# Attention and max-out feed-forward on one core: q and k loaded six tokens to a partition, w1 and w2 loaded over 128 partitions

## The chip, the cores and the metric

The kernel runs on one core of a Trainium2 chip. The metric is the device time of one execution in microseconds. Five executions of the kernel before took 218.94 to 220.14 us, with a median of 219.47 us. In the profile the engines are PE (TensorE, the matrix engine; PEld is its weight load), DVE (VectorE), ACT (ScalarE), POOL (GpSimd) and SP (SyncE, which here only issues DMAs). An engine's name with a q (SPq, PEq) stands for its instruction queue.

## What is computed

The inputs are q, k and v of shape [4, 8, 768, 64] (batch, heads, tokens, head size), three weight matrices, and a flag for each head. A flagged head attends causally to all earlier tokens. Any other head sees only the first 4 tokens and a window of 64. In this draw three of the eight heads are flagged (0, 2 and 6). All data is float32.

```python
def _attn_ref(q, k, v, is_retrieval, n_sink, window):
    scores = scale * np.matmul(q, k.transpose(0, 1, 3, 2))
    ...
    stream_keep = causal & (is_sink | in_win)
    ...
    a = np.exp(scores)
    a = a / (np.sum(a, axis=-1, keepdims=True) + 1e-09)
    return np.matmul(a, v).astype(np.float32)

def _moe_ref(x, w1, w2, w_out):
    return (np.maximum(x @ w1, x @ w2) @ w_out).astype(np.float32)
```

Between the two, the attention output is laid out as x with 4 * 768 = 3072 rows of tokens and 8 * 64 = 512 columns, head h in columns 64h to 64h + 63. w1 and w2 are [512, 1024], w_out is [1024, 512].

## The kernel before, in words

**The order of the heads.** The kernel sorts the heads on the chip (lines 280 to 295): the flagged ones first. Each *slot* 0 to 7 then holds a head, and `perm` holds which. If at most three heads are flagged (they are, here), the first branch at line 672 runs: SP loads the eight head numbers into registers (line 673), and the function `run` works on slots, slots 0 to 2 with the full causal triangle and 3 to 7 with the narrow band. Every load of q, k and v is addressed by the register of its slot (line 541). So the x that the attention writes has its columns in the order of the slots, and the rows of w1 and w2 are loaded in that same order (line 366), 64 rows at a time, each half into 64 partitions.

**Attention.** The function `pair` treats two slots of one batch; there are 4 batches of 4 pairs, 16 pairs. A pair loads q, k and v with two DMAs each (96 DMAs of 192 KB). The load puts token n * 128 + p on partition p, so a partition receives six separate rows of 64 floats. POOL casts each tile to bf16 (line 555; `qb` for q and k, line 574 `vb` for v). PE transposes q and k in six blocks of 128 tokens (line 563) into a PSUM bank (`mm`), and DVE or ACT copies the bank to `qt` (line 567, one copy) and `kz` (line 572, one copy for each head). The helper `copy` records these copies as line 255 on DVE and POOL, and as line 253 on ACT. Then, for each head, come scores on PE (line 435), the exponential on ACT (442), the mask product on DVE (451), the product with v on PE (507, 517), and the normalisation on DVE (524, 525), which writes the head's 64 columns of `xs`. After both heads of a pair, PE transposes the pair's 128 columns (601) and a copy puts them in `xt` (603).

**Feed-forward.** max(a, b) is computed as relu(a - b) + b. So `wd_bf` = w1 - w2 (line 384), and `wm_bf` = w2 @ w_out, which is made once on PE (lines 393 and 404). For each batch, in two halves of 384 tokens, `dense` computes relu(x @ wd) (lines 617, 624, 626), and then x @ wm + relu(...) @ w_out into one PSUM bank (636 and 642), copies it out (646) and stores it (649). `dense(b)` waits for all four `xt` copies of its batch and for the prepared weights.

**What sets the order.** Nothing is scheduled at run time: `Plan` holds a list of operations, each with its cost on the engines that may do it, a priority, the buffers it needs and the operations it waits for, and `schedule` (line 65) simulates them in time. It gives each operation to an engine and emits all of them in the order of their planned starts. Each engine, and SP's queue of DMA issues, then runs its instructions in exactly that order. A planned DMA takes its size over its `rate`; the loads of q, k and v are planned at 0.225 (MB per us), w1 and w2 at 0.37. The loads of pair r have priority r, and the 16 loads of w1 and w2 have 2.5, so they stand between the loads of pairs 2 and 3. Nine `ld` tiles take the loads of three pairs. PSUM has three `sc` banks, two `po` and three `mm`; the transposes, the feed-forward and the preparation of the weights share the three `mm` banks.

Of the kernel before, what the change touches and what calls it, by code (L numbers as in the profile page):

```python
# [149 lines left out]
def kernel(  # L150
# [61 lines left out]
    perm = tl("perm", [128, H + 4], I32)  # L212
    nsf = tl("nsf", [128, H], F32)
# [52 lines left out]
    with tc.manual_schedule():  # L266
# [27 lines left out]
        V.tensor_copy(out=perm[:, H:H + 1], in_=nr)  # L294
        V.tensor_scalar_mul(out=far0, in0=far, scalar1=nsink)

    def run(full, head, rows, flags):
# [59 lines left out]
        def weights(prio):  # L357
            for i, name in enumerate(("w2", "w1")):
                for c in range(4):
                    for hh in (range(2) if rows else (None,)):  # L360
                        def f(e, name=name, c=c, hh=hh):
                            if hh is None:
                                load_weight(name, c)
                            else:
                                arr = {"w1": moe_w1, "w2": moe_w2}[name].rearrange("(h d) f -> h d f", d=D)
                                nc.sync.dma_start(  # L366
                                    out=w_raw[{"w1": 0, "w2": 1}[name]][64 * hh:64 * hh + 64, c, :],
                                    in_=arr[bass.ds(head(2 * c + hh), 1)].rearrange("o d f -> (o d) f"))
                        d_w[name, c, hh or 0] = P.op(
                            f, {"SP": 0.5}, prio=prio + 0.1 * i + 0.01 * c,  # L370
                            size=0.524 if hh is None else 0.262, rate=0.37)
            return {(n, c): [o for (a, x, _), o in d_w.items() if (a, x) == (n, c)] for n in ("w1", "w2") for c in range(4)}
# [56 lines left out]
        xs, xt, xt_ops = {}, {}, {}  # L429
# [24 lines left out]
        def head_ops(b, s, hh, qt, kz, vb, tops, ov, sink, r):  # L454
# [67 lines left out]
            def norm(e):  # L522
                p3 = po.t[:, 0:NB * (D + 1)].rearrange("p (n e) -> p n e", e=D + 1)
                V.reciprocal(out=rz.t, in_=p3[:, :, D])
                V.tensor_tensor(out=xs[b].t[:, :, s * D:(s + 1) * D], in0=p3[:, :, 0:D],  # L525
                                in1=rz.t.unsqueeze(2).to_broadcast([128, NB, D]), op=ALU.mult)
            return P.op(norm, {"DVE": 0.68}, [prev], [po, rz, xs[b]], prio=hr)

        def pair(b, p):
            r = b * HP + p  # L530
            s0 = 2 * p
            if p == 0:
                xs[b], xt[b], xt_ops[b] = Buf(xs_p), Buf(xt_p), []
            raws, loads = [], []
            for i, src in enumerate((q, k, v)):
                t = Buf(ld)
                raws.append(t)
                if rows:
                    two = []
                    for hh in range(2):  # L540
                        two.append(P.op(lambda e, t=t, src=src, hh=hh: nc.sync.dma_start(  # L541
                            out=t.t[:, hh], in_=src[b, bass.ds(head(s0 + hh), 1)].rearrange(
                                "o (n p) d -> p (o n) d", p=128)),
                            {"SP": 0.5}, (), [t], prio=r + 0.01 * i, size=0.197, rate=0.225))
                    loads.append(two)
                else:
                    loads.append([P.op(lambda e, t=t, src=src: nc.sync.dma_start(
                        out=t.t, in_=src[b, s0:s0 + 2].rearrange("h (n p) d -> p h n d", p=128)),
                        {"SP": 0.45}, (), [t], prio=r + 0.01 * i, size=0.393, rate=0.225)])
# [3 lines left out]
            for i in range(2):  # L553
# [12 lines left out]
                if i == 0:  # L566
                    tops.append(P.op(lambda e, bk=bk: copy(e, qt.t, bk.t.bitcast(BF16)[:, 0:S]),
                                     {"DVE": 0.475, "ACT": 0.69}, [o], [bk, qt], prio=r))
                else:
                    for hh in range(2):  # L570
                        kops.append(P.op(lambda e, bk=bk, hh=hh: copy(
                            e, kz.t[64 * hh:64 * hh + 64, hh, :], bk.t.bitcast(BF16)[64 * hh:64 * hh + 64, 0:S]),
                            {"DVE": 0.475, "ACT": 0.69}, [o] + init, [bk, kz], prio=r + 0.1 * hh))
# [140 lines left out]
```

## Time and profile before

| what | value |
|---|---|
| median of 5 executions | 219.47 us |
| the profiled execution | 219.0 us |
| its span in the profile | 217.1 us |
| mean granted PE clock | 0.97 of full speed |
| busy: PE, ACT, DVE, POOL | 186.0, 136.3, 102.9, 60.1 us |
| DMA packets, and those under 512 B | 81263, 76112 |
| loads of q, k and v | 96 DMAs of 192 KB, 18.9 MB |
| loads of w1 and w2 | 16 DMAs of 256 KB, 4.2 MB |
| copies from PSUM to `kz`, DVE and ACT | 17 of 551 ns, 15 of 793 ns |
| copies from PSUM to `qt`, DVE and ACT | 12 of 552 ns, 4 of 809 ns |

The profile covers the span; 1.9 us of the profiled execution lie outside it. A busy time is the union of an engine's instructions, and for matrix products the ends are modelled. Where a copy has two lines in the profile (253 and 255), the tile's name says which copy it is.

### The profile page before, as it was taken

Reading aid. Unit: us, or ns where it says so; the run is one execution under the profiler, and the core shown is the slowest. Engines: PE = TensorE matmul, PEld = TensorE weight load, DVE = VectorE, ACT = ScalarE, POOL = GpSimd, SP = SyncE. Lnnn points to the kernel's source line nnn. Section 1 sums busy time; section 2 is a strip of 40 time slices with the busy share of each in tenths; the row PEclk is TensorE's granted clock in tenths of the full one; section 3 lists DMA queues with packets and bytes.
Section 4 is the critical chain, followed back from the end, with each engine's and each line's share of the span. In section 5 each row is a group of like instructions: output and inputs, shape, how many; then the busy total and the mean of one; then the engine's idle time right before and its main releaser. Section 6 shows DMA issues by size and latency. Waiting matters only on the chain.

```text
span 217.1 us, 4707 instructions
## 1 busy us (share of the span) xinstructions
PE 186.0 (86%) x1700; PEld 117.0 (54%) x1700; DVE 102.9 (47%) x269; ACT 136.3 (63%) x262; POOL 60.1 (28%) x117
## 2 busy tenths in 40 slices
PE   0029767699789998999999999999999999999990
PEld 0027546535567776667676677645445454554540
DVE  3886867532978898969898468400000000000000
ACT  0739878427988988978998887625436262442621
POOL 1473420656446455644636200000000000000000
PEclk9999995769999999999999999999999999999997
DMA  5999999999999999999996111012021121202121
GB/s 168 312 222 219 221 246 248 228 194 222 219 194 226 180 225 202 224 226 227 234 238 145 51 50 51 2 53 97 0 97 48 61 87 46 100 3 97 48 91 66
DMA packets 81263, 31.85 MB, mean 147 GB/s; under 512 B 76112, under 2 KB 76112, under 8 KB 81232
## 3 DMA queue, kind: packets, MB, share of 16 engines
q1 hardware_dynamic: 81232, 31.47, 64.9%
q8 instruction: 15, 0.25, 0.5%
q14 instruction: 16, 0.13, 0.2%
HBM read 25.17 MB, written 6.29 MB: 145 GB/s over the span
## 4 chain that ended last, share of the span: by engine, by line
PE 55%; DMA 14%; SPq 11%; DVE 5%; ACT 5%; issue 4%; POOL 3%; POOLq 0%; ACTq 0%; DVEq 0%
PE mm L636 17%; PE mm L617 16%; SPq L541 9%; PE mm L642 8%; DMA raw<-in_moe_w_dram 7%; PE sc L435 6%; DMA ld<-in_v_dram 3%; PE po L507 3%; DMA ld<-in_k_dram 2%; PE mm L563 2%; ACT at L442 2%; ACT kz L253 2%; DVE kz L255 2%; DMA ir<-in_is_retrieval_dram 1%; SPq L366 1%
## 5 line engine op out<-in xcount | busy, mean ns | idle before, releaser
L636 PE MATMUL mm<-wo_bf,raw 128*128 128x512 bf16 x192 | 46.3, 379 | 0.0
L617 PE MATMUL mm<-xt,wd_bf 128*128 128x384 bf16 x256 | 46.0, 326 | 0.0
L435 PE MATMUL sc<-qt,kz 128*128 128x256 bf16 (+3 forms) x240 | 41.0, 270 | 5.4 <-ACT at L442 2.2
L253 ACT COPY ot<-mm 128x512 f32<-128x512 f32 x22 | 12.9, 585 | 38.4 <-PE mm L642 38.4
L442 ACT ACTIVATE as<-sc 128x384 bf16<-128x384 f32 (+3 forms) x72 | 32.4, 517 | 4.5 <-PE sc L435 4.2
L624 ACT ACTIVATE raw<-mm 128x384 bf16<-128x384 f32 x55 | 27.0, 492 | 8.2 <-PE mm L617 7.8
L255 POOL CAST qb<-ld 128x768 bf16<-128x768 f32 x31 | 26.6, 862 | 19.9 <-DMA ld<-in_k_dram 10.8
L617 PEld LDWEIGHTS <-wd_bf 128*128 128x128 bf16 x256 | 23.8, 98 | 14.3
L563 PE MATMUL mm<-ident,qb 128*128 128x128 bf16 x192 | 17.1, 229 | 15.2 <-POOL qb L255 15.1
L636 PEld LDWEIGHTS <-raw 128*128 128x128 bf16 x192 | 18.3, 98 | 20.0 <-issue 0.6
L435 PEld LDWEIGHTS <-kz 128*128 128x128 bf16 x240 | 20.7, 99 | 15.0 <-issue 7.1
L451 DVE TENSOR_TENSOR as<-as,smk 128x448 bf16<-128x448 bf16 (+2 forms) x60 | 23.0, 420 | 5.6 <-ACT as L442 5.6
L642 PE MATMUL mm<-wm_bf,xt 128*128 128x512 bf16 x96 | 24.6, 379 | 0.0
L563 PEld LDWEIGHTS <-qb 128*128 128x128 bf16 x192 | 13.1, 102 | 18.8 <-POOL qb L255 17.4
L451 DVE TENSOR_TENSOR at<-at,msk 128x512 bf16<-128x512 bf16 (+2 forms) x48 | 18.8, 419 | 4.2 <-ACT at L442 4.0
L442 ACT ACTIVATE at<-sc 128x512 bf16<-128x512 f32 (+1 forms) x36 | 20.5, 570 | 0.4 <-PE sc L435 0.3
L525 DVE TENSOR_TENSOR xs<-po,rz 128x384 bf16<-128x384 f32 x32 | 17.8, 558 | 1.1
L255 POOL CAST vb<-ld 128x768 bf16<-128x768 f32 x16 | 13.5, 845 | 15.9 <-DMA ld<-in_v_dram 8.5
L507 PE MATMUL po<-vb,at 128*128 128x65 bf16 x252 | 15.2, 195 | 2.3 <-DVE at L451 2.0
L253 ACT COPY kz<-mm 64x768 bf16<-64x768 bf16 x15 | 11.9, 793 | 7.3 <-DVE kz L255 6.8
L507 PEld LDWEIGHTS <-at 128*128 128x128 bf16 x252 | 12.6, 99 | 5.0 <-DVE at L451 3.7
L642 PEld LDWEIGHTS <-xt 128*128 128x128 bf16 x96 | 9.1, 98 | 10.2
(74 smaller groups left out, 189.4 us busy)
## 6 DMA issues: line engine op xcount, KB each, us to landing
ld<-in_q_dram SPq DMA_DIRECT2D x32, 192.0 KB, 4.3
ld<-in_k_dram SPq DMA_DIRECT2D x32, 192.0 KB, 4.4
ld<-in_v_dram SPq DMA_DIRECT2D x32, 192.0 KB, 4.4
out_dram<-ot SPq DMA_DIRECT2D x24, 256.0 KB, 2.0
raw<-in_moe_w_dram SPq DMA_DIRECT2D x16, 256.0 KB, 7.6
raw<-in_moe_w_out_dram SPq DMA_DIRECT2D x4, 512.0 KB, 5.4
ir<-in_is_retrieval_dram SPq DMA_DIRECT2D x1, 8.0 KB, 3.1
```

The source lines that it names most:

```text
L253: nc.scalar.copy(out=o, in_=i)
L255: (nc.vector if e == "DVE" else nc.gpsimd).tensor_copy(out=o, in_=i)
L435: nc.tensor.matmul(sc.t[:, off:off + w], lhsT=lhsT(j), rhs=qt.t[:, q0:q0 + w], start=True, stop=True, skip_group_check=True)
L442: nc.scalar.activation(out=view(at.t), in_=view(sc.t), func=ACT.Exp, scale=scale, bias=0.0 if bias is None else bias)
L451: V.tensor_mul(out=a, in0=a, in1=m)
L507: nc.tensor.matmul(po.t[:, i * (D + 1):(i + 1) * (D + 1)], lhsT=at.t[:, off + t * 128:off + (t + 1) * 128], rhs=vb.t[:, hh, j, :], **flag_ ...
L541: two.append(P.op(lambda e, t=t, src=src, hh=hh: nc.sync.dma_start(out=t.t[:, hh], in_=src[b, bass.ds(head(s0 + hh), 1)].rearrange("o (n p ...
L563: nc.tensor.transpose(psb[:, n * 128:(n + 1) * 128], t.t[:, n].rearrange("p h d -> p (h d)"), ident)
L617: nc.tensor.matmul(bk.t[:, 0:GT], lhsT=wd_bf[:, c, f * 128:(f + 1) * 128], rhs=xt[b].t[:, c, g * GT:(g + 1) * GT], start=(c == 0), stop=(c ...
L624: nc.scalar.activation(out=gt.t[:, f, :], in_=bk.t[:, 0:GT], func=ACT.Relu)
L636: nc.tensor.matmul(bk.t, lhsT=gt.t[:, f, t * 128:(t + 1) * 128], rhs=wo_bf[:, f, :], start=(f == 0), stop=False)
L642: nc.tensor.matmul(bk.t, lhsT=xt[b].t[:, c, c0:c0 + 128], rhs=wm_bf[:, c, :], start=False, stop=(c == KC - 1))
```

## The change

**Loads of q and k.** Partition p now receives tokens 6p to 6p + 5, which are 1536 contiguous bytes of the input. v keeps the old order. The rate planned for q and k becomes 0.33.

**Token order.** The transposes then produce, in block n, the tokens n, 6 + n, 12 + n and so on. The copies to `qt` and `kz` put them back: they read the PSUM bank with a stride of 128 elements in the inner loop of six, and write contiguously. Their planned cost becomes 0.93 on DVE and 0.8 on ACT (from 0.475 and 0.69).

**Weights.** w1 and w2 are loaded in their natural order, four DMAs of 512 KB each, all 128 partitions at once, with 4 KB rows; the planned rate becomes 0.36.

**Columns of x.** Since the weights are no longer permuted, x must be in natural order: the normalisation writes its 64 columns of `xs` at an offset that DVE holds in a register. A new tile `pcol` (the head numbers times 64) is computed once, and DVE loads eight registers from it.

**Transposes of x.** A block of 128 columns now holds heads of different pairs, so `x_turn` does the four transposes and four copies of a batch after all eight normalisations of the batch, with the priority of the last pair.

```diff
+        V.tensor_scalar_mul(out=pcol, in0=perm[:, 0:H], scalar1=float(D))
         V.tensor_scalar_mul(out=far0, in0=far, scalar1=nsink)
...
         def weights(prio):
             for i, name in enumerate(("w2", "w1")):
                 for c in range(4):
-                    for hh in (range(2) if rows else (None,)):
...
-                                nc.sync.dma_start(
-                                    out=w_raw[{"w1": 0, "w2": 1}[name]][64 * hh:64 * hh + 64, c, :],
-                                    in_=arr[bass.ds(head(2 * c + hh), 1)].rearrange("o d f -> (o d) f"))
...
+                    d_w[name, c] = P.op(lambda e, name=name, c=c: load_weight(name, c), {"SP": 0.5},
+                                        prio=prio + 0.1 * i + 0.01 * c, size=0.524, rate=0.36)
...
-                V.tensor_tensor(out=xs[b].t[:, :, s * D:(s + 1) * D], in0=p3[:, :, 0:D],
+                V.tensor_tensor(out=xs[b].t[:, :, bass.ds(col(s), D)], in0=p3[:, :, 0:D],
                                 in1=rz.t.unsqueeze(2).to_broadcast([128, NB, D]), op=ALU.mult)
+        def tok(t):
+            return t.rearrange("c (p n) -> c p n", n=NB)
+
+        def blk(t):
+            return t.rearrange("c (n p) -> c p n", p=128)
...
+                order, rate = ("(n p)", 0.225) if src is v else ("(p n)", 0.33)
...
-                                "o (n p) d -> p (o n) d", p=128)),
-                            {"SP": 0.5}, (), [t], prio=r + 0.01 * i, size=0.197, rate=0.225))
+                                f"o {order} d -> p (o n) d", p=128)),
+                            {"SP": 0.5}, (), [t], prio=r + 0.01 * i, size=0.197, rate=rate))
...
-                    tops.append(P.op(lambda e, bk=bk: copy(e, qt.t, bk.t.bitcast(BF16)[:, 0:S]),
-                                     {"DVE": 0.475, "ACT": 0.69}, [o], [bk, qt], prio=r))
+                    tops.append(P.op(lambda e, bk=bk: copy(e, tok(qt.t), blk(bk.t.bitcast(BF16)[:, 0:S])),
+                                     {"DVE": 0.93, "ACT": 0.8}, [o], [bk, qt], prio=r))
...
-                            e, kz.t[64 * hh:64 * hh + 64, hh, :], bk.t.bitcast(BF16)[64 * hh:64 * hh + 64, 0:S]),
-                            {"DVE": 0.475, "ACT": 0.69}, [o] + init, [bk, kz], prio=r + 0.1 * hh))
+                            e, tok(kz.t[64 * hh:64 * hh + 64, hh, :]),
+                            blk(bk.t.bitcast(BF16)[64 * hh:64 * hh + 64, 0:S])),
+                            {"DVE": 0.93, "ACT": 0.8}, [o] + init, [bk, kz], prio=r + 0.1 * hh))
...
+        def x_turn(b):
+            for c in range(KC):
+                bk = Buf(mm_p)
+
+                def xtr(e, c=c, bk=bk):
+                    psb = bk.t.bitcast(BF16)
+                    for n in range(NB):
+                        nc.tensor.transpose(psb[:, n * 128:(n + 1) * 128],
+                                            xs[b].t[:, n, c * 128:(c + 1) * 128], ident)
+                o = P.op(xtr, {"PE": 0.34}, norms[b], [bk, xs[b], xt[b]], prio=100 + 2 * (b * HP + HP - 1) + 0.1 * c)
+                xt_ops[b].append(P.op(lambda e, c=c, bk=bk: copy(e, xt[b].t[:, c, :], bk.t.bitcast(BF16)[:, 0:S]),
+                                      {"DVE": 0.475, "ACT": 0.69}, [o], [bk, xt[b]], prio=20 + 4 * b))
...
                 pair(b, p)
+            x_turn(b)
             dense(b)
...
+        _, xcol = nc.values_load_multi_w_load_instructions(
+            pcol[0:1, 0:H], engines=(mybir.EngineType.DVE,), min_val=0, max_val=(H - 1) * D,
+            skip_runtime_bounds_check_because="a permutation of the heads")
```

## The prediction, made before the changed kernel ran

> **What bounds the kernel now.** I read the slices of the span first (three of the page's rows: PE's busy tenths, its granted clock, the DMA rate).
>
> ```profile
> PE   0029767699789998999999999999999999999990
> ...
> PEclk9999995769999999999999999999999999999997
> ...
> GB/s 168 312 222 219 221 246 248 228 194 222 219 194 226 180 225 202 224 226 227 234 238 145 51 50 51 2 53 97 0 97 48 61 87 46 100 3 97 48 91 66
> ```
>
> A slice is 5.4 us. PE has holes up to the eleventh slice (60 us), and nearly none later, until its last product at 212.3 us. DMA moves about 220 GB/s until slice 21 (115 us) and has little to do after. So the end is set by PE, and PE loses its time before 60 us. The loss there is larger than the holes: the clock is granted at 0.5 to 0.7 in slices 7 to 9.
>
> Next, stretches of my choice: length, busy time of PE, PEld, DVE, ACT and POOL, the granted clock, the DMA share, GB/s.
>
> ```profile
> 5.40:8.50 3.10, 0.00 (x0) 0.00 (x0) 2.48 (x7) 1.57 (x2) 1.51 (x5) 1.00 1.02 380
> ...
> 28.00:33.00 5.00, 2.74 (x35) 1.70 (x34) 2.59 (x9) 3.99 (x8) 1.17 (x5) 1.00 1.04 247
> 33.00:38.00 5.00, 4.04 (x47) 3.29 (x46) 3.82 (x12) 4.39 (x9) 0.00 (x0) 0.56 1.05 247
> 50.00:60.00 10.00, 8.73 (x99) 5.65 (x98) 6.53 (x15) 8.71 (x17) 5.87 (x10) 1.00 1.29 218
> 60.00:90.00 30.00, 28.29 (x368) 21.18 (x367) 26.11 (x66) 26.70 (x54) 16.50 (x32) 1.00 1.04 207
> ```
>
> The first row is mostly w_out: 128 partitions, 2 KB rows, 380 GB/s. The next two hold w1 and w2: 4 KB rows in 64 partitions, 247. The fourth holds loads of q, k and v alone: 256 B rows, 218. The DMA share is 1 throughout, so these are rates of a full DMA. In the last row DVE and ACT are busy 87% and 89%, which matters below.
>
> Last, the chain of waits (start, length, what), where PE is starved.
>
> ```profile
> 26.42 0.50 SPq L366
> 27.12 6.72 DMA raw<-in_moe_w_dram
> 33.87 8.49 DMA raw<-in_moe_w_dram
> 42.49 2.36 POOL wd_bf L384
> 44.85 1.05 SPq L541
> 46.09 3.75 DMA ld<-in_v_dram
> 49.98 0.83 POOL vb L255
> ```
>
> The end hangs on the transfer of w1 and w2, which stands in front of pair 3's loads. Pair 3 completes batch 0, and only then is there feed-forward work for PE. The first such product in the timeline:
>
> ```profile
> 60.41 0.56 DVE L255 COPY xt<-mm 128x768 bf16<-128x768 bf16 x1 [0.27 <-PE mm L601]
> ...
> 61.23 0.81 PE L617 MATMUL mm<-xt,wd_bf 128*128 128x384 bf16 x4
> ```
>
> From 61.1 to 139.6 us PE is busy 75.2 of 78.5 us, with attention and feed-forward mixed; from 139.6 to 212.3 it is busy 72.6 of 72.7 us with feed-forward alone. So an early start of the feed-forward moves the end by as much, unless the mixed stage gets less dense.
>
> **The change, part by part.** The sum is against the profiled execution, 219.0 us (span 217.1 and 1.9 outside), which is 0.5 below the median.
>
> *Start.* `pcol` is one small DVE instruction ahead of far0, on which SP's first load waits; a like one (line 287) takes 0.17 us. **+0.2.** DVE also loads eight registers; SP's load of eight (line 673) takes 0.55 us. That delays the masks, which end at 15.0 before a DVE hole of 0.7: nothing, or 0.5 if the first copy of kz comes earlier than now.
>
> *q and k of pairs 0 to 2.* 12 DMAs, 2.36 MB, take 10.8 us at 218 GB/s. Rows of 1536 B are not in the trace: the ends are 218 (256 B, no gain) and 380 (2 KB). I take 350, near the 2 KB row: 6.7 us. SP issues no faster than one load each 0.58 us, though (7.64, 8.22, 8.80 in the chain): 12 take 7.0. **-3.8** (0 to -3.8).
>
> *w1 and w2.* 4.19 MB at 247 GB/s take 17.0 us. At w_out's 380 they take 11.0. **-6.0**, with nothing as the other end, if 4 KB rows are slow for another reason than the 64 partitions. SP also issues 8 DMAs fewer.
>
> *q and k of pair 3.* 0.79 MB, 3.6 us to 2.2: **-1.4** (0 to -1.5). So pair 3's v is cast at 49.98 - 11.0 = 39.0 us, if nothing but DMA holds it. Attention of pairs 0 to 2 and the weights' preparation must fit in: DVE and ACT are busy 65% and 69% from 10 to 60 us (32.6 and 34.6 us in the windows of 10 us), so they have the room.
>
> *Copies of q and k.* There are 3 a pair, 48 in all. For a strided read of PSUM the trace has no row. Its lower end is today's 0.55 us on DVE and 0.80 on ACT. On DVE the f32 copies grow from 0.551 (384 elements, line 626) to 0.692 (512, `ot`), 1.1 ns an element; carried to 768 that is 0.97. I take 0.97 on DVE; on ACT, where f32 grows from 0.492 to 0.585 and so gives 0.77 at 768, no more than today's 0.80. The upper end is ACT as much dearer as DVE: 1.4. For pair 3 a `qt` and a `kz` copy lie on the path: **+0.8** (0 to 1.2).
>
> [...]
>
> [...]
>
> *x_turn.* Before, one transposition group and one copy followed a batch's last normalisation; now four do. A group is 0.34 us on PE, a copy 0.55 (DVE) or 0.81 (ACT). Three more copies on two engines: **+1.5** for batch 0 (0.8, if both engines are free, to 4, if attention of the next batch goes first: these copies have priority 20, that attention 8 to 16). Later batches have feed-forward of the batch before to cover it: 72.7 us of it are still to do when the last attention ends, so batch 3 costs nothing.
>
> First feed-forward: 39.0 + (61.1 - 50.0) + 0.8 + 1.5 = 52.4, that is **-8.7**, the start's +0.2 in it.
>
> *More attention done by then.* After pair 3 a pair's loads take 0.79/0.35 + 0.39/0.218 = 4.1 us instead of 5.4, so pairs 4 and 5 are further on: **-1.0** (0 to -3).
>
> *The mixed stage.* 36 copies of q and k lie in it. With half on DVE, 18 * 0.42 = 7.6 us more, on engines that are busy 87%. PE, which is the bound, has feed-forward to do meanwhile. I charge **+1.5** (0 to 10, if every one on DVE made PE wait).
>
> *Registers.* SP's dynamic loads show 37 + 29 ns of register work each; for 32 normalisations on DVE that is 2.1 us. **+0.4** (0 to 2).
>
> *POOL and SP.* POOL waits 8.8 us for w1 at 38 us, with pair 3's casts queued behind; part of the shift above, not counted again. Faster loads free the `ld` tiles only as fast as POOL casts: 3 a pair, 2.5 us of 4.1. It fits.
>
> Sum: -8.7 - 1.0 + 1.5 + 0.4 = -7.8, which is 211.2 us against 219.0, and 211.7 against the median. I say **211.5**.
>
> **The rivals.**
>
> *A. The gain is made and mostly given back.* In batch 1 the loads no longer throttle attention, DVE and ACT are full, and PE waits for relu outputs (priority 15 and up, behind that attention). For: 87% busy already, and 7.6 us more. Against: from batch 2 on relu goes first. Price: 4 pairs, about 22 us, with PE at 75% instead of 95%, 4.4 us more: 216; with the copies at the upper ends 218.
>
> *B. Slower: the copies become the bound.* If a strided copy takes 1.9 us on either engine, 1.2 more than the mean of today, the 36 in the mixed stage add 43 us on two engines, 22 us, of which feed-forward on PE can cover little, since relu and output copies need the same two engines. With half of it on PE's path: 11 us there, and 12 copies before, 12 * 1.2 / 2 = 7 more, against a gain of 10.1 without the copies (7.8 + 0.8 + 1.5): 227. The point from which it decides is 0.67 us more for each copy (36 * 0.67 / 4 + 12 * 0.67 / 2 = 10). Nothing in the profile shows strided reads that dear. At 0.8 it is 221.
>
> *C. The change doesn't do what it says.* 1536 B rows stay near 218 GB/s and the weights near 247. The transfers gain nothing, and the additions cost 0.2 + 0.8 + 1.5 + 1.5 + 0.4: 223. Against it: the 380 of the 2 KB rows.
>
> *D. More gain.* The clock stays full, and the weights' preparation is out of pair 3's way (2.7 us of line 404 lie between 50 and 55 us): 205.
>
> **Chances.** The forecast, 207 to 215: 0.56. A: 0.18, mostly below 219. B: 0.08. C: 0.08. D: 0.10. Differences under 0.3% can't be told from none. Faster is the forecast, D and most of A: 0.80; within 0.3% some of A: 0.04; slower B, C: 0.16. The range from 204.5 to 219.5 leaves out B, C and some of D, under 2 in 10.
>
> **What would show it.** Right: rates over 300 GB/s in slices 3 to 7; `wd_bf` before 38 us; first line 617 product near 52; `kz` copies near 0.97 us on DVE and 0.8 on ACT; the feed-forward alone still at 13 us a half batch (the chain has 5.20 for line 617 and three times 1.73 + 0.86); q and k landing in about 3 us instead of 4.3. Wrong: a first 617 product near 52 with an unchanged end (A), copies over 1.2 us (B), or q and k issues still 0.7 us long with the queue full (C). The largest doubts are the 247 of the weights, whose cause I don't know, and the order that the planner makes of new costs.

## The result: no gain, and the profile after

The changed kernel takes 219.92 us (median of 52 runs), the kernel before 219.44 (median of 94). The ratio is 1.0026, with a 95% interval of 1.0014 to 1.0038: slower by a quarter of a per cent, and so, for all purposes, no gain. The forecast was 211.5 us, in a range that ended at 219.5. It was wrong by 8.4 us. A ratio here always compares undisturbed runs alone; one kernel below has too few of them for a ratio.

The profiled execution took 219.85 us, with a span of 218.1. The slices of the changed kernel (PE, its granted clock, GB/s):

```profile
PE   0049655998878999988999999999999999999992
...
PEclk9999996799999999999999999999999999999999
...
GB/s 173 313 305 339 391 404 296 284 198 267 235 213 218 256 205 235 258 154 51 2 0 3 48 51 50 3 51 101 0 96 48 51 98 0 96 51 73 71 51 104
```

The loads kept their promise: slices 2 to 6 move 305 to 404 GB/s, and the loads are over in slice 18 (by 98 us), before in slice 22 (by 119 us). Yet PE's hole in slices 6 and 7 (27 to 38 us) has become deeper, 5 and 5 tenths where it was 6 and 7. Stretches of the same kernel (length, busy time of PE, PEld, DVE, ACT, POOL, granted clock, DMA share, GB/s):

```profile
20.00:25.00 5.00, 4.05 (x59) 2.81 (x58) 4.54 (x11) 4.49 (x9) 3.09 (x8) 1.00 1.05 368
25.00:30.00 5.00, 3.51 (x39) 2.04 (x38) 4.90 (x13) 4.95 (x11) 0.59 (x2) 1.00 1.02 409
30.00:35.00 5.00, 0.63 (x8) 0.42 (x8) 5.00 (x3) 1.77 (x4) 4.89 (x3) 0.89 1.07 352
35.00:40.00 5.00, 4.54 (x52) 4.34 (x51) 4.08 (x9) 2.23 (x6) 2.50 (x5) 0.50 1.00 288
...
50.00:60.00 10.00, 8.51 (x100) 5.90 (x101) 8.08 (x18) 7.68 (x15) 5.38 (x11) 1.00 0.91 244
60.00:90.00 30.00, 27.27 (x332) 18.57 (x330) 25.85 (x57) 25.93 (x52) 16.13 (x31) 1.00 0.82 228
```

The fourth column tells the story. DVE is busy 4.54, 4.90 and 5.00 of 5 us from 20 to 35 us. In the third row it is busy all the time with *three* instructions, and PE does 0.63 us of work. Before, DVE was busy 2.59 and 3.82 in 28 to 33 and 33 to 38 us.

The first feed-forward product, which the forecast put at 52.4 and which was at 61.2 before, now is at 65.4. From the timeline of the changed kernel (start, length, engine, line):

```profile
63.68 0.55 DVE L256 COPY xt<-mm 128x768 bf16<-128x768 bf16 x1
64.09 0.83 ACT L254 COPY xt<-mm 128x768 bf16<-128x768 bf16 x1
64.48 0.55 DVE L256 COPY xt<-mm 128x768 bf16<-128x768 bf16 x1
65.37 0.81 PE L618 MATMUL mm<-xt,wd_bf 128*128 128x384 bf16 x4
```

The chain of waits up to that product has no transfer left in it (before, w1, w2 and v took 19 us of it), but this:

```profile
29.99 5.49 DVE as L443 x3
...
44.72 0.96 DVE kz L256
...
49.20 0.97 DVE as L443
50.18 0.87 DVE kz L256
51.13 0.79 ACT kz L254
...
64.23 0.69 ACT xt L254
```

So the bound has moved from the transfers to DVE, and in part to ACT: masks (`as`) of 5.49 us for three, strided copies (`kz`), and the late copies of x_turn (`xt`).

A sum that holds for every kernel here is read from two windows, up to the first feed-forward product and from there: the span is the start of that product, PE's busy time after it, and PE's idle time after it (the 4 to 5 us from its last product to the end of the span among it).

| kernel | first product | PE busy after | PE idle after | span |
|---|---|---|---|---|
| before | 61.2 | 147.7 | 8.2 | 217.1 |
| changed | 65.4 | 145.2 | 7.5 | 218.1 |
| contiguous_copies | 64.2 | 143.7 | 6.2 | 214.1 |
| no_subtraction | 59.5 | 144.6 | 8.3 | 212.4 |
| x_turn_first | 62.5 | 144.8 | 6.5 | 213.8 |
| x_turn_first_contiguous | 61.7 | 143.9 | 5.3 | 210.9 |
| weights_and_x_turn_first | 62.9 | 144.6 | 4.8 | 212.3 |

The changed kernel loses 4.2 us at the start of the feed-forward, and gets 2.5 back because more attention is done by then, and 0.7 in idle time. A first product that comes later by x does not make the end later by x.

### The profile page after: what moved, and what is told of

Same layout as the page of the kernel before. It is cut to its first block, busy times and chain, and to the rows that moved or that the text cites. A ratio compares the mean times of both kernels' runs of the same rounds, so it can differ in the third digit from the quotient of the medians.

```text
span 218.1 us, 4700 instructions
## 1 busy us (share of the span) xinstructions
PE 185.9 (85%) x1700; PEld 117.2 (54%) x1700; DVE 113.4 (52%) x264; ACT 139.1 (64%) x268; POOL 58.3 (27%) x117
## 3 DMA queue, kind: packets, MB, share of 16 engines
q1 hardware_dynamic: 40144, 31.47, 46.3%
## 4 chain that ended last, share of the span: by engine, by line
PE 59%; DVE 18%; ACT 13%; issue 5%; POOL 0%; DVEq 0%; ACTq 0%; POOLq 0%
PE mm L637 17%; PE mm L618 16%; PE mm L643 9%; PE sc L427 8%; DVE as L443 4%; DVE kz L256 4%; ACT kz L254 4%; ACT as L434 4%; PE po L499 3%; PE mm L562 3%; DVE at L443 3%; ACT at L434 3%; DVE xs L517 2%; DVE msk L330 1%; PE mm L396 1%
## 5 line engine op out<-in xcount | busy, mean ns | idle before, releaser
L637 PE MATMUL mm<-wo_bf,raw 128*128 128x512 bf16 x192 | 46.3, 379 | 0.1
L443 DVE TENSOR_TENSOR as<-as,smk 128x448 bf16<-128x448 bf16 (+2 forms) x60 | 28.0, 498 | 8.2 <-ACT as L434 8.0
L427 PEld LDWEIGHTS <-kz 128*128 128x128 bf16 x240 | 21.7, 102 | 13.7 <-issue 5.2
L256 POOL CAST qb<-ld 128x768 bf16<-128x768 f32 x30 | 25.6, 871 | 12.2 <-PE mm L562 5.9
L562 PE MATMUL mm<-ident,qb 128*128 128x128 bf16 x192 | 16.2, 230 | 13.1 <-POOL qb L256 11.8
L562 PEld LDWEIGHTS <-qb 128*128 128x128 bf16 x192 | 13.3, 103 | 15.1 <-POOL qb L256 11.7
L443 DVE TENSOR_TENSOR at<-at,msk 128x512 bf16<-128x512 bf16 (+2 forms) x48 | 17.7, 402 | 5.0 <-ACT at L434 4.6
L254 ACT COPY kz<-mm 64x768 bf16<-64x768 bf16 x16 | 12.7, 791 | 11.3 <-DVE kz L256 9.4
L517 DVE TENSOR_TENSOR xs<-po,rz 128x384 f32 x32 | 17.8, 558 | 1.2
L499 PE MATMUL po<-vb,as 128*128 128x65 bf16 x220 | 13.5, 199 | 5.8 <-DVE as L443 5.5
L256 DVE COPY kz<-mm 64x768 bf16<-64x768 bf16 x16 | 15.2, 952 | 5.1 <-PE mm L562 2.7
L499 PE MATMUL po<-vb,at 128*128 128x65 bf16 x252 | 14.3, 195 | 2.7 <-DVE at L443 2.1
```

What stands on the lines that cost most here:

```text
L254: nc.scalar.copy(out=o, in_=i)
L256: (nc.vector if e == "DVE" else nc.gpsimd).tensor_copy(out=o, in_=i)
L427: nc.tensor.matmul(sc.t[:, off:off + w], lhsT=lhsT(j), rhs=qt.t[:, q0:q0 + w], start=True, stop=True, skip_group_check=True)
L443: V.tensor_mul(out=a, in0=a, in1=m)
L499: nc.tensor.matmul(po.t[:, i * (D + 1):(i + 1) * (D + 1)], lhsT=at.t[:, off + t * 128:off + (t + 1) * 128], rhs=vb.t[:, hh, j, :], **flag_ ...
L517: V.tensor_tensor(out=xs[b].t[:, :, bass.ds(col(s), D)], in0=p3[:, :, 0:D], in1=rz.t.unsqueeze(2).to_broadcast([128, NB, D]), op=ALU.mult)
```

## The experiments

The theories. **(1)** POOL's subtractions w1 - w2 now run beside the masks of attention on DVE, and collide with them. **(2)** x_turn, at its low priority, holds the first product back. **(3)** The strided copies cost more than I charged. **(4)** DVE, ACT and PE, in their fixed order, are the bound before the first product, so faster loads cannot bring it much forward. The forecast's own theory is that the transfers are the bound.

Two kinds of kernel have to be kept apart. Some keep the changed kernel's (or the old kernel's) order of instructions, and differ only in the edit. Others change a planned cost, a priority or a list of operations, so the planner makes a new order. I measured what a new order alone is worth only at the end, and it changes how the rest is read, so it comes first.

**What the order alone is worth.** Two kernels that do exactly the work of before, with one planned number changed.

```diff
-            return P.op(norm, {"DVE": 0.68}, [prev], [po, rz, xs[b]], prio=hr)
+            return P.op(norm, {"DVE": 0.70}, [prev], [po, rz, xs[b]], prio=hr)
```

> The kernel before with one planned cost changed (a normalisation planned at 0.70 us instead of 0.68), and so another order of the same work; the planner's own end moves by -0.17 us. It measures how much a time may move by the order alone. If parts of the change can be read from kernels that were planned anew, it stays within 1 us of 219.4. If the order alone is worth as much as the parts that do not add up, it moves by 2 us or more, and differences of that size between planned-anew kernels say nothing about a part.

```diff
-                            {"SP": 0.5}, (), [t], prio=r + 0.01 * i, size=0.197, rate=0.225))
+                            {"SP": 0.5}, (), [t], prio=r + 0.01 * i, size=0.197, rate=0.22))
```

> The kernel before with one planned number changed (loads of q, k and v planned at 220 GB/s instead of 225), so another order of the same work; the planner's own end moves by +0.14 us. A second sample of what the order alone is worth, beside replan_norm (+0.44%, first feed-forward product 2.4 us later). Within 1 us of 219.4 if that is the size of it; 2 us or more away if order effects are as large as the misfit between the single parts.

Measured: 220.48 us, ratio 1.0044 (1.0018 to 1.0070), and 224.47 us, ratio 1.0198 (1.0148 to 1.0248). First products at 63.6 and 64.9 (the second from its slowest execution, of 227.55 us). The second missed its expectation by far: a change of 2% in one planned number costs 4.3 us by the ratio. A wider pair stands among the kernels below: w_natural_with_x_turn and weights_and_x_turn_first do the same loads, copies, products and transposes, planned with other costs, rates and priorities, and take 226.99 and 213.12 us. That is 13.9 us for another order and another division of the work between DVE and ACT. So **a difference of a few us between kernels that were planned anew proves nothing about a part.** What is called shown below rests on the kernels with one order.

### One part changed, the order kept

**The subtractions, moved.** All four on DVE.

```diff
-                o.emit(o.engine)
+                o.emit("DVE" if o in wd_ops else o.engine)
```

> The changed kernel, same planned order, but all four subtractions w1 - w2 run on DVE; two of them stood on POOL. Theory 1 (the gain of the loads is lost because POOL's two subtractions, 2.35 us each from 29.6 to 34.4 us, hold three DVE masks up: 2.28, 2.1 and 1.2 us where 0.43 is usual): the masks go back to about 0.43 us, DVE gets 2 x 1.22 us instead of some 4 us of stretching, POOL casts pair 3 from 30 us on, the first product of line 618 comes 2 to 4 us before 65.4, and the time falls to 216 to 218 us. Theory 2 (the gain is lost in x_turn and in the slower copies): the masks get shorter and nothing follows, 219.5 to 220.5 us.

Measured: 219.46 us, ratio 1.0001 (0.9974 to 1.0027), first product 64.5. The masks do get short again, but DVE now does four subtractions itself, in the stretch in which it is already full:

```profile
29.91 0.89 DVE L443 TENSOR_TENSOR as<-as,smk 128x448 bf16<-128x448 bf16 x3
...
34.56 3.60 DVE L376 TENSOR_TENSOR wd_bf<-raw 128x1024 bf16<-128x1024 f32 x2
```

POOL's two casts beside the second row take 2.72 us together, 1.82 in the changed kernel. So theory 1, that the gain comes back when the work is put on DVE, falls: the time hardly moves.

**The subtractions, left out.** The same order, and the feed-forward reads w2's bf16 copy.

```diff
-                (V if e == "DVE" else nc.gpsimd).tensor_sub(
-                    out=wd_bf[:, c, :], in0=w_raw[0][:, c, :], in1=w_raw[1][:, c, :])
+                return
...
-                            nc.tensor.matmul(bk.t[:, 0:GT], lhsT=wd_bf[:, c, f * 128:(f + 1) * 128],
+                            nc.tensor.matmul(bk.t[:, 0:GT], lhsT=w2_bf[:, c, f * 128:(f + 1) * 128],
```

> The changed kernel in the same order, but w1 - w2 is left out: the first feed-forward products read w2's bf16 copy instead, and the four subtractions (two on POOL, two on DVE) do nothing. It takes away the stretch of 2.3 to 2.5 us that each mask takes on DVE while POOL subtracts, the two subtractions on DVE, and POOL's 4.8 us ahead of pair 3's casts. If the stretch from pair 3's v cast to the first product is long because DVE and POOL are full there and PE's order cannot go around them, pair 2's last normalisation comes near 39 us (43.2 in the changed kernel), the first product at 58 to 61 us (65.4) and the time falls to 214 to 217 us. If the fixed order is held up by something else (PE's own order, x_turn), the first product stays at 63.5 or later and the time over 218.

Measured: 214.42 us, ratio 0.9798 (0.9739 to 0.9857), first product 59.5. Pair 2's last normalisation ends at 37.1 instead of 43.2, pair 3's k is transposed at 38.2 instead of 44.1. Here is how the collision looks. First the last masks of pairs 0 to 2 on DVE and then POOL in the timeline of before, then POOL and the masks in the changed kernel, and the masks without the subtractions. Before:

```profile
35.25 1.69 DVE L451 TENSOR_TENSOR as<-as,smk 128x448 bf16<-128x448 bf16 x6
...
38.17 2.35 POOL L384 TENSOR_TENSOR wd_bf<-raw 128x1024 bf16<-128x1024 f32 x1 [8.84 <-DMA raw<-in_moe_w_dram]
42.49 2.35 POOL L384 TENSOR_TENSOR wd_bf<-raw 128x1024 bf16<-128x1024 f32 x1 [1.97 <-DMA raw<-in_moe_w_dram]
45.95 0.82 POOL L255 CAST qb<-ld 128x768 bf16<-128x768 f32 x1 [1.10 <-DMA ld<-in_q_dram]
```

The changed kernel, POOL:

```profile
29.59 4.80 POOL L376 TENSOR_TENSOR wd_bf<-raw 128x1024 bf16<-128x1024 f32 x2 [3.69 <-DMA raw<-in_moe_w_dram]
34.34 1.82 POOL L256 CAST qb<-ld 128x768 bf16<-128x768 f32 x2
36.71 0.83 POOL L256 CAST vb<-ld 128x768 bf16<-128x768 f32 x1 [0.55 <-DMA ld<-in_v_dram]
```

The changed kernel, DVE:

```profile
29.90 5.56 DVE L443 TENSOR_TENSOR as<-as,smk 128x448 bf16<-128x448 bf16 x3
```

Without the subtractions, DVE:

```profile
29.82 0.89 DVE L442 TENSOR_TENSOR as<-as,smk 128x448 bf16<-128x448 bf16 x3
```

Three masks take 0.89 us, or 5.56 (2.28, 2.50 and 0.94) beside two subtractions on POOL and the start of a cast. Before, the same subtractions ran from 38 to 45 us: the last masks of pairs 0 to 2 were done by 37, pair 3 had not come in, so they met no mask. The wait for the loads had been their cover. Note that this kernel takes work away as well (two subtractions on DVE) and that PE's clock before the first product was granted at 1.00 (0.95 in the changed kernel), so I take 5.5 us as an upper bound for the subtractions. With the same loads and the same order, less work on DVE and POOL brings the first product 5.9 us forward: that is theory 4, with DVE and POOL as the engines, for this part of the stretch.

**The copies, contiguous.** The token order is not restored.

```diff
-                    tops.append(P.op(lambda e, bk=bk: copy(e, tok(qt.t), blk(bk.t.bitcast(BF16)[:, 0:S])),
+                    tops.append(P.op(lambda e, bk=bk: copy(e, qt.t, bk.t.bitcast(BF16)[:, 0:S]),
...
```

> The changed kernel, same planned order, but the copies to qt and kz read the bank contiguously, as before the change (the tokens of q and k then stay permuted, so the attention is not the reference's; the work is the same otherwise). 22 DVE copies go from 0.95 to 0.55 us, ACT's stay at 0.80. Theory 3 (the slower DVE copies ate the gain): DVE gets 8.8 us back, some 2.5 us of it before the first product, and the time falls by 2.5 to 5 us, to 215 to 217.5. Theories 1 and 2: 0.5 to 1 us less, 219 to 219.5.

Measured: 215.15 us, ratio to before 0.9810 (0.9764 to 0.9857), so 4.8 us less than the changed kernel. The first product is only 1.2 us earlier (64.2); the rest comes from the mixed stage, where the last normalisation of attention ends at 137.8 instead of 142.1.

**Only the strided reads, in the kernel before.** Its loads and its order stay, so tokens come out mixed.

```diff
-                    tops.append(P.op(lambda e, bk=bk: copy(e, qt.t, bk.t.bitcast(BF16)[:, 0:S]),
+                    tops.append(P.op(lambda e, bk=bk: copy(e, tok(qt.t), blk(bk.t.bitcast(BF16)[:, 0:S])),
...
```

> The kernel before, same planned order, with only the strided reading in the copies to qt and kz (the loads are as before, so the tokens are permuted and the attention is not the reference's). 29 of the 48 copies are on DVE there, 0.40 us more each, 11.6 us in all. If their price is that of the changed kernel (4.8 us for 22 copies): 224 to 226. If the kernel before waits for data while DVE is free (its DVE is 65% busy up to 60 us): 220.5 to 222.

Measured: 225.79 us, ratio 1.0284 (1.0245 to 1.0323). The first product stays (61.7), the last normalisation of attention ends at 145.4 instead of 138.8: all of it is in the mixed stage. Theory 3 holds in both kernels. The groups of costliest lines have the price of one (busy, then mean ns), in the changed kernel:

```profile
L254 ACT COPY kz<-mm 64x768 bf16<-64x768 bf16 x16 | 12.7, 791 | 11.3 <-DVE kz L256 9.4
...
L256 DVE COPY kz<-mm 64x768 bf16<-64x768 bf16 x16 | 15.2, 952 | 5.1 <-PE mm L562 2.7
```

0.95 us on DVE, 0.79 on ACT: on ACT this strided read costs nothing (0.793 before), and on DVE it is nearly the 0.97 of the forecast. The size of a copy was right, and what it does to the stage was not.

**The rows, short again.**

```diff
-                order, rate = ("(n p)", 0.225) if src is v else ("(p n)", 0.33)
+                order, rate = "(n p)", 0.225 if src is v else 0.33
```

> The changed kernel, same planned order, but q and k are loaded as before, one 256 B row for each token (with the strided copies the tokens are then permuted, so the attention is not the reference's). This prices the longer rows alone. If PE's late start is set by the transfers, as I forecast, the first product moves by the 5 us that the forecast counted for q and k, and the time rises to 224 or 225. If the engines behind the loads are the bound, as the profile after suggests (DMA share 0.77 to 0.92 from 40 us on), pairs 0 to 2 come up to 3.8 us later and part of it is waited out: 220.5 to 222.5.

Measured: 220.62 us, ratio 1.0020 (0.9980 to 1.0060). The long rows of q and k are worth 0.7 us by the medians and nothing by the ratios, though they cut the DMA engines' time from 53.3% of 218.8 us to 46.3% of 218.1, that is by 15.6 us. Pair 3's v and the first product with short rows:

```profile
40.58 0.91 POOL L256 CAST vb<-ld 128x768 bf16<-128x768 f32 x1 [0.29 <-DMA ld<-in_v_dram]
...
65.75 0.81 PE L618 MATMUL mm<-xt,wd_bf 128*128 128x384 bf16 x4
```

In one and the same order, pair 3's v is cast 3.9 us later (36.71 in the changed kernel) and the first product comes 0.4 us later. That is the plainest sign that the transfers are no longer the bound in the changed kernel.

### Parts, planned anew

**x_turn alone**, in the kernel before (its weights and columns stay in the order of the slots).

```diff
-            norms = [head_ops(b, s0 + hh, hh, qt, kz, vb, tops + [kops[hh]], ov, sink, r) for hh in range(2)]
...
+            norms[b] += [head_ops(b, s0 + hh, hh, qt, kz, vb, tops + [kops[hh]], ov, sink, r) for hh in range(2)]
...
+            x_turn(b)
             dense(b)
```

> The kernel before, with only x_turn of the change: the four transposes and copies of a batch stand behind its eight normalisations; weights and columns stay in the order of the slots, so the result is the reference's. Theory 2 (x_turn costs 5 us at batch 0, as the profile after shows 6.3 us from the last normalisation to the first product where it was 1.3): the first product comes 3 to 5 us after 61.1 and the time rises to 221 to 223 us. Theories 1 and 3: attention goes on meanwhile, so the end moves by less than 1 us, 219.5 to 220.5.

Measured: 224.27 us (four runs, 221.5 to 226.4), first product 63.3: slower, by 2 us at least, but within what an order can do.

**The wide loads of w1 and w2 alone.** The rows of the weights and the columns of x do not match.

```diff
-                    for hh in (range(2) if rows else (None,)):
...
+                    d_w[name, c] = P.op(lambda e, name=name, c=c: load_weight(name, c), {"SP": 0.5},
+                                        prio=prio + 0.1 * i + 0.01 * c, size=0.524, rate=0.36)
```

> The kernel before, with only the loads of w1 and w2 of the change: four DMAs each, 128 partitions, natural order. x keeps the order of the slots, so rows and columns no longer match and the output is not the reference's; the work is the same otherwise. If the costs found so far add up (strided copies 4.8, x_turn 4.7, longer rows of q and k -0.7, the whole +0.4 us), the wide loads are worth the rest, 8.4 us: 211 us. If they don't add up, because the feed-forward waits for the latest of several things, less: my forecast counted 6.0 us for it; with pair 3's loads 6 us earlier and the same engines behind them I expect 3 to 5 us, 215 to 217.

Measured: 218.80 us, ratio 0.9973 (0.9946 to 0.9999), above what was expected. In the profiled execution, with 216.09 us the fastest of eleven (the others took 217.8 to 219.6), pair 3's v is cast at 43.4 (50.0 before) and the first product comes at 57.2 (61.2 before): in this order 4.0 of 6.6 us do reach the first product. The same with columns by register and x_turn:

```diff
+                V.tensor_tensor(out=xs[b].t[:, :, bass.ds(col(s), D)], in0=p3[:, :, 0:D],
...
+            x_turn(b)
             dense(b)
```

> The kernel before, with the wide loads of w1 and w2, the columns of x by register and x_turn; q and k and their copies as before. The result is the reference's. By the sum of parts (wide loads minus 3 to 8, x_turn plus 4.7): 216 to 221 us, and since it is the changed kernel without the strided copies and the longer rows, it should be near the 215.15 us of the run with contiguous copies plus 0.7 for the rows: 216.

Measured: 226.99 us, ratio 1.0340 (1.0290 to 1.0390), first product 66.0. It has less of the change than the changed kernel and is 7 us slower than it, and 13.9 us slower than weights_and_x_turn_first, which does the same work: the clearest sign of the orders' part.

**The loads of q and k alone**, with contiguous copies, and with the copies that restore the order (there with a planned rate of 0.30).

```diff
-                                "o (n p) d -> p (o n) d", p=128)),
-                            {"SP": 0.5}, (), [t], prio=r + 0.01 * i, size=0.197, rate=0.225))
+                                f"o {order} d -> p (o n) d", p=128)),
+                            {"SP": 0.5}, (), [t], prio=r + 0.01 * i, size=0.197, rate=rate))
```

> The kernel before, with only the change's loads of q and k, copies contiguous (tokens permuted, so the attention is not the reference's). If the rows bring 0.7 us as in the changed kernel: 218.5 to 219.5. If transfers set the start of the feed-forward in this order, 4 to 5 us: 214.5 to 216.

```diff
+                    tops.append(P.op(lambda e, bk=bk: copy(e, tok(qt.t), blk(bk.t.bitcast(BF16)[:, 0:S])),
+                                     {"DVE": 0.93, "ACT": 0.8}, [o], [bk, qt], prio=r))
...
```

> The kernel before, with the change's loads of q and k and the copies that restore the token order (planned rate of these loads 0.30); weights, columns and transposes of x as before. The result is the reference's. If the copies cost what they cost in the changed kernel (4.8 us) and the rows bring 0.7: 223 to 224 us. If the rows bring more here, because the slow weights still stand between pairs 2 and 3 and everything ahead of them comes 4 us earlier: 219 to 221.

Measured: 219.34 us, ratio 0.9980 (0.9951 to 1.0009), and 219.88 us, ratio 0.9981 (0.9941 to 1.0021). Neither can be told from no change, and the second does not show the 4.8 to 6.2 us that the strided copies cost where the order is kept. In the first, pair 3's v is cast at 45.2 (50.0 before), and the first product stays where it was (61.5, and 61.2 before).

**Both loads, none of the costs**: the wide loads of w1 and w2 and the long rows of q and k, in the kernel before, without columns by register, x_turn and restoring copies.

```diff
+                    d_w[name, c] = P.op(lambda e, name=name, c=c: load_weight(name, c), {"SP": 0.5},
+                                        prio=prio + 0.1 * i + 0.01 * c, size=0.524, rate=0.36)
...
+                order, rate = ("(n p)", 0.225) if src is v else ("(p n)", 0.30)
...
```

> The kernel before with both loads of the change (1536 B rows for q and k, planned at 0.30; w1 and w2 over 128 partitions) and none of what they need: contiguous copies, x in slot order, transposes pair by pair. Tokens and rows then no longer match, so the output is not the reference's; it is the ceiling of what the loads can give. My forecast's theory, that the transfers set the start of the feed-forward: 11 us less, 208 to 210 us. Theory 4, that from about 10 to 40 us DVE, ACT and PE's fixed order are the bound as soon as the data come earlier (each load alone gave 0.2 to 0.8 us): 215.5 to 218.5 us.

Measured: 220.71 us, ratio 1.0069 (1.0047 to 1.0090), first product 59.8, though pair 3's v is cast at 37.5 (50.0 before). 12.5 us earlier data brought the first product forward by 1.4. In it POOL subtracts at 29.7 to 34.6 and two masks take 4.88 us, much as in the changed kernel. The time is above both expected ranges and proves little, given the orders. The gap between 12.5 and 1.4 is more than one changed number moved the first product by (2.4 and 3.7). So the forecast's theory, that the first product follows the data one for one, falls: in four orders 4.8, 6.6, 12.5 and 13.3 us of earlier data (the last is the changed kernel, with its dearer copies and x_turn) went with a first product 0.3 later, 4.0 earlier, 1.4 earlier and 4.2 later. Theory 4 fits that best; how much of each is the engines' work and how much the order stays open.

**Pair 3 ahead of the weights' products** on PE, in the changed kernel (`later` holds the eight product groups of w2 and w_out).

```diff
+                if r == 3:
+                    for x in later:
+                        x.deps.append(o)
```

> The changed kernel, with all eight product groups of w2 * w_out (6.9 us of PE) made to wait for pair 3's transposes, so that PE's order has pair 3 first. If these weight products in PE's order are what holds pair 3 up, its transposes come at about 41 us instead of 42.9 and 44.1 and the first product 2 to 3 us earlier, and the time is 217 to 218.5. If DVE's masks and copies hold pair 3 up, PE only waits elsewhere: transposes within 1 us of the changed kernel's, and the time within 1.5 us of its 219.9. The planner, by its own costs, plans the first product 2.7 us later than in the changed kernel and the end 1.9 us later, so a slower time is possible as well.

Measured: 220.88 us, ratio 1.0054 (1.0013 to 1.0096). Pair 3's transposes come at 41.6 and 42.0 (42.9 and 44.1), the first product at 65.6. Pair 2's last normalisation ends at 42.7 (43.2). So PE's order held pair 3's transposes up by 1 to 2 us, more than the 1 us that was allowed for, but not the first product.

### Versions that are faster than both

**x_turn earlier in the plan**, first with the rest of the change as it is, then with all subtractions on DVE.

```diff
-                o = P.op(xtr, {"PE": 0.34}, norms[b], [bk, xs[b], xt[b]], prio=100 + 2 * (b * HP + HP - 1) + 0.1 * c)
+                o = P.op(xtr, {"PE": 0.34}, norms[b], [bk, xs[b], xt[b]], prio=2 * (b * HP + HP - 1) + 0.1 * c)
...
-                                      {"DVE": 0.475, "ACT": 0.69}, [o], [bk, xt[b]], prio=20 + 4 * b))
+                                      {"DVE": 0.475, "ACT": 0.69}, [o], [bk, xt[b]], prio=8 * b + 6))
```

> The changed kernel with x_turn at the priority of the batch's own attention: its transposes at 2 * (4b + 3) instead of 100 more, its copies at 8b + 6 instead of 20 + 4b. Theory 2 (x_turn's price comes from waiting behind the next batch's attention, 6.3 us from the last normalisation to the first product): that stretch falls to 3 to 5 us and the time to 217.5 to 219. If the price is that all four groups and copies wait for the latest of eight heads, whatever their priority: 219.5 to 220.5.

```diff
-                o.emit(o.engine)
+                o.emit("DVE" if o in wd_ops else o.engine)
```

> The kernel of x_turn_first with the four subtractions w1 - w2 on DVE, in the same order. As that one, and POOL no longer holds up DVE's masks and pair 3's casts: 0.5 us less than x_turn_first as in wd_on_dve, 217 to 218.5. Above 219.5 if both are off the path that decides.

Measured: 216.35 us, ratio 0.9857 (0.9810 to 0.9903), and 217.11 us, ratio 0.9887 (0.9850 to 0.9925). From the last normalisation to the first product it is 4.5 us in the first, 6.3 in the changed kernel. The first is faster than was expected, but its order is a new one, so the 3.6 us are not shown to be x_turn's. All subtractions on DVE bring nothing in this order either.

**With contiguous copies as well**, in the order of x_turn_first.

```diff
-                    tops.append(P.op(lambda e, bk=bk: copy(e, tok(qt.t), blk(bk.t.bitcast(BF16)[:, 0:S])),
+                    tops.append(P.op(lambda e, bk=bk: copy(e, qt.t, bk.t.bitcast(BF16)[:, 0:S]),
...
```

> The changed kernel with x_turn's work put earlier in the plan (as x_turn_first, same order), and with the copies of q and k reading PSUM contiguously, so that the token order is not restored and the output has mixed tokens. If the strided copies cost 4 to 5 us in any order, it comes to 211 to 213 us (216.4 with strided copies); then the loads with a good order and without their dearer copies would have given about what was forecast. If the gains overlap, it stays at 214 to 216.

Measured: 212.38 us, ratio 0.9666 (0.9625 to 0.9706), the middle of what was expected. Against x_turn_first the order is the same, and the strided copies cost 4.0 us once more.

**Without the half on q and k**, in the order of x_turn_first: q and k in 256 B rows and contiguous copies, as before; the wide weights, the columns by register and x_turn stay.

```diff
-                order, rate = ("(n p)", 0.225) if src is v else ("(p n)", 0.33)
+                order, rate = "(n p)", 0.225 if src is v else 0.33
...
-                    tops.append(P.op(lambda e, bk=bk: copy(e, tok(qt.t), blk(bk.t.bitcast(BF16)[:, 0:S])),
+                    tops.append(P.op(lambda e, bk=bk: copy(e, qt.t, bk.t.bitcast(BF16)[:, 0:S]),
...
```

> The changed kernel without its half on q and k: they load in 256 B rows as before and are copied contiguously, while the wide loads of w1 and w2, the columns by register and x_turn stay, with x_turn's work earlier in the plan; the order is that of x_turn_first. If the long rows earn 0.7 us (as short_rows says) and the strided copies cost 4 to 5 us in any order, it comes to 212 to 214 us (216.4 with both, 212.4 with long rows and contiguous copies), the best kernel that computes the whole reference. If the long rows matter more with this order, it is 215 or more.

Measured: **213.12 us, ratio 0.9716 (0.9691 to 0.9742)**, as expected, and 2.8% less than the kernel before. What part of that is the weights' loads and what part a lucky order is not shown: the same work in the order of w_natural_with_x_turn takes 226.99 us. Its slices:

```profile
PE   0039674898879999999999999999999999999992
...
PEclk9999999579999999999999999999999999999999
...
GB/s 164 320 267 263 312 409 280 267 190 265 259 226 265 238 265 228 276 271 160 2 3 49 10 91 5 2 91 64 5 108 35 85 68 48 100 3 99 49 52 107
```

Only slices 2 (mostly w_out), 5 and 6 (w1 and w2) are over 300 GB/s, and PE has no hole after slice 12. It does not start the feed-forward earlier than the kernel before (62.9 against 61.2): PE has more of the attention behind it by then (144.6 us busy after it, not 147.7) and idles less later (4.8, not 8.2).

## Why the prediction was wrong, point by point

- **The loads: right.** Slices 3 to 7 were to be over 300 GB/s: 3 to 6 are, and 7 is at 296. q and k land 3.6 and 3.5 us after the issue (4.3 and 4.4 before); I had said about 3. Pair 3's v is cast at 36.7, where I had 39.0. The rate of the long rows was a little high: 15.6 us less for 12.58 MB, which at 218 GB/s takes 57.7, leaves 42.1 us, an estimated 299 GB/s, where I took 350.
- **"So they have the room": the step that failed.** DVE and ACT were busy 65% and 69% from 10 to 60 us, and I took that mean for room at the place where it was needed. Faster loads bring the same work into 10 to 40 us, where DVE is now busy 27.3 of 30 us (21.3 before; 24.1 without the subtractions), and the idle time in the mean was the wait for the loads itself: from 38.7 to 50 us DVE was busy 4.8 of 11.3 us before. From pair 3's v cast to the first product I had kept the 11.1 us of before, with 0.8 and 1.5 added: 13.4. It is 28.7. Of the 17.5 us more than before (11.2 in these rows), 8.3 pass before pair 3's k is transposed (a thing that had come 0.9 us ahead of v's cast and now comes 7.4 behind it), 4.3 from there to its last normalisation, and 4.9 from there to the first product. Without the subtractions k is transposed 2.0 us behind v's cast, which takes away 5.4 of the 8.3; the 4.3 and the 4.9 stay. What makes the 4.3 is open (contiguous copies bring the first product 1.2 forward).
- **The subtractions: not in the sum at all.** I named POOL's wait for w1 as part of the shift, and did not ask what its work would meet once the wait was gone. It meets the masks. At most 5.5 us of the time.
- **The copies: +0.8 and +1.5 (the mixed stage), measured 4 to 6 together.** My 0.42 us a copy was right (0.40), and 10 was my upper end for the mixed stage. The argument that PE has feed-forward to do meanwhile did not hold: 22 copies on DVE in the changed kernel, 0.40 us each, are 8.8 us, and 4.8 of them reach the end; in strided_copies_alone it is 6.2 of 11.6 (29 copies).
- **x_turn: +1.5, measured 4.9** from the last normalisation to the first product; 0.8 to 4 were my bounds. The reason was the one that I gave for the upper end: attention of the next batch goes first. An earlier place in the plan comes with 3.6 us less, in another order.
- **The end follows the first product: only in part.** 4.2 us later there, 1.0 at the end.
- **Rivals.** A (made and mostly given back) named the right place for part of it, full DVE and ACT, but has the first product near 52. B (copies over 1.2 us) and C (no faster loads) are excluded by 0.95 us and 368 to 409 GB/s. D (a full clock, the weights' preparation out of the way) has neither: the clock is granted at 0.50 from 35 to 40 us, and products of w2 and w_out still run at 50 to 54. That the gain does not arise at all, because the engines take the transfers' place as the bound before the first product, was not among them.
- **The planner's order: a doubt without a term.** I named it among the largest doubts and put nothing in the sum for it. Orders of the same work differ by 1.0, 4.3 and 13.9 us here, so it may hold much of the missing 8.4.

The terms together: with x_turn early and the copies contiguous the kernel takes 212.4 us. The forecast less its 2.3 us for the copies is 209.2, so some 3 us are left for the subtractions' collision and the slower rate. That is a sum that would fit and no proof, since this order is not the changed kernel's. Shown in the changed kernel's own order are three things: the copies cost 4.8 us, the subtractions at most 5.5, and later loads of q and k next to nothing. What stays open is why single parts planned anew do not add up; the order alone is enough to explain it, which does not show it for each kernel.

## What to carry to other kernels

When a transfer is the bound, look at what the engines do *while* they wait for it: work that hides in that wait (here two subtractions on POOL) lands on someone else's path as soon as the wait is gone, and a mean busy share over the whole stretch says nothing about that. Count a stage like the one here, with DVE 87% and ACT 89% busy (60 to 90 us before), as full when work is added to it: dearer copies in strided_copies_alone, an estimated 11.6 us more on DVE (29 copies), moved the end by 6.2. And where a planner sets a fixed order, measure a mere change of one planned number first: here it was worth 0.4 and 2%, and two orders of the same work were 6% apart, more than any part of the change.

## What the runs showed of the hardware

- In the changed kernel two mask products on DVE with both inputs in SBUF, of 0.32 to 0.39 us each before (28 to 38 us), took 2.28 and 2.50 us while POOL subtracted (2.34 us an instruction), and two others 0.94 and 0.97 us (at 34.5 and 49.2 us) while POOL cast (two casts in 1.82 and in 1.88 us). Three in a row took 5.56 us beside two subtractions of 4.80 us together and the start of a cast, and 0.89 us where the subtractions were left out. Why a mask took about as long as a subtraction is not shown.
- A strided 16-bit read of PSUM (768 elements, step 128 in the inner loop) cost DVE 0.95 us (changed kernel, `kz`) instead of 0.55 (before), and ACT 0.79 in both.
- Loads of w1 and w2 over 128 partitions (4 KB rows, 512 KB a DMA) moved 368 to 409 GB/s (20 to 30 us of the changed kernel); in two halves of 64 partitions it had been 247 (28 to 38 us of the kernel before).
